# Loading the first batch's q and k as float32 on SyncE, with the casts on chip, in an opening whose order is written anew

## The chip, the cores and the metric

The kernel runs on one core of a Trainium2 chip. Its metric is device time in microseconds of that core, the median of several executions. Engines are named as in the profile: PE (TensorE, matmuls; PEld its weight loads), DVE (VectorE), ACT (ScalarE), POOL (GpSimd), SP (SyncE, which here only issues DMAs).

## The reference

A causal attention with a sliding window of 64 keys over 8 batches, 8 heads, 576 positions and 64 columns a head; its output, as 4608 rows of 512, goes through two dense layers with a gate between them.

```python
scores = scale * q @ k^T                       # scale = 1/8
mask   = (rel >= 0) & (rel < 64)               # rel = row - column
attn   = exp(scores - max) / (sum + 1e-9)      # softmax over masked scores
x      = (attn @ v)  -> (B*S, H*D) = (4608, 512)
h      = x @ w_in                              # 512 -> 2048
g      = h * cos(h)
out    = g @ w_out                             # 2048 -> 512
```

All inputs and the output are float32 in HBM.

## The kernel before

The rows are taken in nine token tiles of 512. For a tile the kernel computes the scores of blocks of 64 rows against the two 64-key chunks that the window touches, the softmax, the value products (`o_ps`, transposed, so that they are the first layer's input `xT`), the first layer in 16 blocks of 128 columns (`h_ps`, L453), the sine (L595) and the gate (L598), and the second layer (`out_ps`, L609). From the second tile on, the attention of a later batch is woven into a tile's two layers: steps are put on a plan with a due time (`at`) and released as the matmuls advance (`pump`).

The opening, up to the first L453 of the second tile, is different. All instructions are issued in program order to the engines' queues (`manual_schedule`), and for the opening that order is the text `FIRST`: a list of step names, each run through the table `steps`. A name carries its arguments, and a last letter `d`, `a`, `p` or `s` says the engine: DVE, ACT, POOL or an SP transfer. The names that matter here:

- `Lq0.p`, `Lk0.p`: load q or k of batch 0 for the pair p of heads. In the kernel before, pair 0 comes as float32 through SP (`load_plain`, L168 to L171) and is cast by `cq`, `ck` (`cast_plain`, the copy itself recorded at L137); pairs 1 to 3 come through POOL, whose DMA casts on the way (`load_heads`, L165). `Lq1`, `Lk1` do the latter for batch 1, `Lv0.c`, `Lv1.c` (L188) load chunks of v, `Lwi.i` and `Lwo.i` quarters of the weights (L204, L207), `Lq2`, `Lk2` chunks of batch 2 (L182).
- `tq`, `tk`, `Tq`, `Tk`: transposes of a pair's rows on PE (L216), put into SBUF by `pq`, `pk`, `Pq`, `Pk` (the copies at L137, or L234 and L236).
- `s`, `m`, `e`, `i`, `n`, `w`, `c`: scores of a group of four row blocks, their maximum, exps (L336), reciprocal, norm (L353), PE transposes (`tw_ps`, L364) and the copy of these (`wT`, L137), for the first tile's eight groups `p.g`. `Gs`, `Gm`, `Ge`, `Gi`, `Gn`, `Gw`, `Gp` are the same for groups 8 to 18, of the second tile; for most of these `Gc` takes the place of `Gw` and `Gp`: a DMA transpose through SP (L367).
- `zA`, `zB`, `zC`, `yA`, `yB`, `y`: the spreading of v's chunks to both halves of the partitions (`spread_v`): a copy, or with `s` an SP transfer (L199).
- `v`, `x`: value products of the first tile, by halves (L403), and their put into `xT`; `h`, `S`, `g`: first layer, sine and gate of the first tile, by halves (L417, L423, L429); `o.q.m`: a quarter of the second layer for 128 rows (L436), `oc` its put; `V`, `X`: value products (L384) and their put for the second tile.
- `ms`: clearing of a pair's block tile `qB` (L546); `io`, `mk`, `mc`: the masks; `tb`, `tb2`: loads of ScalarE's tables.

Every engine works through its own instructions in the order in which the list issued them, and waits there for what each needs.

Of the kernel before, what the change touches and what calls it, by code (L numbers as in the profile page):

```python
# [75 lines left out]
def kernel(  # L76
# [572 lines left out]
```

## Time and profile before

| what | before |
|---|---|
| time, median of 3 runs | 309.11 us (309.06 to 309.75) |
| span of the profiled execution | 306.25 us |
| what lies around the span in that execution (time less span) | 2.86 us, a time of 309.11 us |
| busy share of the span | PE 97%, ACT 76%, DVE 75%, POOL 63% |
| granted PE clock | 1.00 in the stretches read |
| HBM read, written | 36.70 MB, 9.44 MB |

Times in profile rows count from the start of the span. A row of the timeline has its start, its length (of several instructions of one kind in a run, from the first's start to the last's end), the engine, the line, the operation with output and inputs, and in brackets the idle time just before it with what ended it. A row of groups has busy time and mean of one in ns. Since instructions are pipelined, neighbouring rows can overlap a little.

### The profile page before, as it was taken

The numbers are of one execution on the slowest core, as the hardware profiler recorded it, in microseconds if no ns is written. First come the engines' busy times: TensorE is split into PE (matmuls) and PEld (weight loads), VectorE is DVE, ScalarE is ACT, GpSimd is POOL, SyncE is SP. The second block draws the span as 40 slices with busy tenths as digits, with TensorE's granted clock in tenths as the row PEclk, the third lists the DMA queues.
The fourth block names the chain that finished last, engine by engine and source line by source line (L and its number), as shares of the span: only waits on it lengthen the run. The fifth ranks groups of instructions, "written<-read, shape, count | busy, mean of one in ns | idle before, by whom it ended". The sixth has DMA issues, their size and how long they took to land.

```text
span 306.3 us, 7904 instructions
## 1 busy us (share of the span) xinstructions
PE 296.2 (97%) x2616; PEld 159.0 (52%) x2616; DVE 228.5 (75%) x908; ACT 234.3 (76%) x785; POOL 192.5 (63%) x228
## 2 busy tenths in 40 slices
PE   3889999999999999999999999999999999999996
PEld 2768844545555555445544555454545554454443
DVE  5999978599769976798579857986698668235801
ACT  5998799677997799779976997699879986116600
POOL 8998579995659669967998599959903930000000
PEclk9999999999999999999999999999999999999999
DMA  7999999999999995999999999999794643011011
GB/s 146 179 212 192 200 180 130 121 149 191 226 113 116 175 223 80 121 133 232 125 121 137 231 143 104 157 221 148 86 137 107 169 78 141 2 68 71 1 67 70
DMA packets 159945, 42.14 MB, mean 138 GB/s; under 512 B 148256, under 2 KB 155168, under 8 KB 159904
## 3 DMA queue, kind: packets, MB, share of 16 engines
q0 software_dynamic: 100192, 18.06, 80.1%
q1 hardware_dynamic: 59568, 23.38, 40.6%
q8 instruction: 20, 0.33, 0.4%
q14 instruction: 21, 0.17, 0.2%
q10 hardware_dynamic: 144, 0.20, 0.2%
HBM read 36.70 MB, written 9.44 MB: 151 GB/s over the span
## 4 chain that ended last, share of the span: by engine, by line
PE 90%; POOL 4%; DMA 2%; DVE 1%; ACT 1%; issue 1%; POOLq 0%; DVEq 0%; ACTq 0%
PE h_ps L453 35%; PE out_ps L609 35%; PE h_ps L417 5%; PE s_ps L303 4%; PE out_ps L436 4%; PE o_ps L384 3%; DMA k<-in_k_dram 2%; POOL w L353 2%; PE tq_ps L219 1%; POOL v L188 1%; PE out_ps L465 1%; PE s_ps L309 1%; PE tw_ps L364 1%; POOL w_in L204 1%; ACT e L336 1%
## 5 line engine op out<-in xcount | busy, mean ns | idle before, releaser
L609 PE MATMUL out_ps<-w_out,gT 128*128 128x512 bf16 x496 | 117.3, 379 | 0.0
L453 PE MATMUL h_ps<-xT,w_in 128*128 128x512 bf16 x512 | 115.3, 379 | 0.3
L595 ACT ACTIVATE sin<-h_ps 128x512 f32<-128x512 f32 x128 | 73.7, 598 | 32.7 <-PE h_ps L453 31.4
L598 DVE TENSOR_TENSOR gT<-h_ps,sin 128x512 bf16<-128x512 f32 x128 | 82.1, 685 | 21.9 <-ACT sin L595 21.2
L336 ACT ACTIVATE e<-s,negm 128x128 f32<-128x128 f32 (+1 forms) x256 | 97.1, 382 | 0.6 <-DVE negm L324 0.6
L353 POOL TENSOR_TENSOR w<-e,rden 128x512 bf16<-128x512 f32 (+1 forms) x74 | 70.0, 962 | 36.6 <-DVE rden L346 18.8
L453 PEld LDWEIGHTS <-w_in 128*128 128x128 bf16 x512 | 48.8, 98 | 54.7 <-issue 0.4
L609 PEld LDWEIGHTS <-gT 128*128 128x128 bf16 x496 | 45.9, 98 | 44.2
L324 DVE CUSTOM_DVE_ANT_0 s<-s_ps,mask 128x128 f32<-128x128 f32 (+1 forms) x256 | 56.4, 279 | 1.7 <-PE s_ps L309 0.9
L336 ACT ACTIVATION_READ_ACCUMULATOR e<-s,negm 128x1 f32 x256 | 48.3, 189 | 0.0
L182 POOL DMA_DIRECT2D q<-in_q_dram x36 | 28.3, 785 | 10.7 <-DMA q<-in_q_dram 4.0
L188 POOL DMA_DIRECT2D v<-in_v_dram x40 | 34.4, 878 | 0.3 <-issue 0.2
L182 POOL DMA_DIRECT2D k<-in_k_dram x36 | 28.2, 783 | 3.9 <-DMA k<-in_k_dram 1.2
L137 ACT COPY out_sb<-out_ps 128x512 f32<-128x512 f32 (+1 forms) x18 | 10.2, 566 | 24.5 <-PE out_ps L609 18.4
L346 DVE RECIPROCAL rden<-den 128x4 f32<-128x4 f32 (+1 forms) x79 | 13.1, 166 | 19.0 <-ACT e L336 18.6
L303 PEld LDWEIGHTS <-qB 128*128 128x128 bf16 x216 | 16.5, 98 | 14.2
L137 DVE CAST xT<-o_ps 128x512 bf16<-128x512 f32 x24 | 15.5, 677 | 10.1 <-PE o_ps L384 10.1
L137 DVE COPY out_sb<-out_ps 128x512 f32<-128x512 f32 x18 | 12.4, 690 | 13.2 <-PE out_ps L609 12.5
L324 DVE DVE_READ_ACCUMULATOR2_ANT negm<- 128x1 f32 x256 | 21.3, 83 | 0.0
L303 PE MATMUL s_ps<-kT,qB 128*128 128x128 bf16 (+1 forms) x216 | 21.2, 216 | 0.0
L137 POOL COPY v<-v 64x1536 bf16<-64x1536 bf16 (+3 forms) x12 | 18.8, 1570 | 0.3
L137 DVE COPY qB<-tq_ps 64x384 bf16<-64x384 bf16 (+1 forms) x40 | 15.6, 390 | 0.4
(70 smaller groups left out, 257.8 us busy)
## 6 DMA issues: line engine op xcount, KB each, us to landing
out_dram<-out_sb SPq DMA_DIRECT2D x16, 512.0 KB, 7.5
v<-in_v_dram POOLq DMA_DIRECT2D x32, 128.0 KB, 5.7
q<-in_q_dram POOLq DMA_DIRECT2D x36, 96.0 KB, 8.6
k<-in_k_dram POOLq DMA_DIRECT2D x36, 96.0 KB, 8.5
w_in<-in_moe_w_in_dram POOLq DMA_DIRECT2D x4, 512.0 KB, 8.7
w_out<-in_moe_w_out_dram POOLq DMA_DIRECT2D x4, 512.0 KB, 10.8
wT<-w SPq DMA_TRANSPOSE x68, 4.4
q<-in_q_dram POOLq DMA_DIRECT2D x7, 144.0 KB, 6.0
```

The lines of the kernel that those rows point to most:

```text
L137: {"a": nc.scalar.copy, "p": nc.gpsimd.tensor_copy}.get(engine, nc.vector.tensor_copy)(out, in_)
L182: nc.gpsimd.dma_start(out=st[name, b][:, c].rearrange("p (h d) -> p h d", h=H), in_=src.rearrange("h p d -> p h d"))
L188: nc.gpsimd.dma_start(out=vt.rearrange("p (h d) -> p h d", h=H), in_=v[b, :, c * 128:c * 128 + n, :].rearrange("h p d -> p h d"))
L303: nc.tensor.matmul(out=s_ps[:, u, 0:64 * chunks].rearrange("p (a t) -> p a t", a=chunks), lhsT=qblocks[(b % 2) * PAIRS + p][:, j].rearrang ...
L324: nc.vector.tensor_tensor_reduce(out=s[:, u, c], in0=s_ps[:, u, c], in1=mask[:, 2 - j % 2 if j else 0, c], scale=-scale if b else -1.0, sc ...
L336: nc.scalar.activation(e[:, u, c], s[:, u, c], AF.Exp, bias=negm[:, u:u + 1], scale=1.0 if n < n_first else -1.0, accum_out=den[:, u:u + 1])
L353: (nc.gpsimd if engine == "p" else nc.vector).tensor_tensor(out=w[:, 0:u], in0=e[:, 0:u], op=ALU.mult, in1=rden[:, 0:u].unsqueeze(2).to_br ...
L417: nc.tensor.matmul(out=h_ps[:, half * e:half * e + half], lhsT=w_in_sb[:, ks, ff * 128:ff * 128 + 128], rhs=st["xT", 0][:, ks, half * g:ha ...
L453: nc.tensor.matmul(out=st["h", ff], lhsT=w_in_sb[:, ks, ff * 128:ff * 128 + 128], rhs=st["xT", mt][:, ks], start=start, stop=stop)
L595: nc.scalar.activation(sin, h_ps, AF.Sin, bias=math.pi / 2.0)
L598: nc.vector.tensor_tensor(out=gt[:, e], in0=h_ps, in1=sin, op=ALU.mult)
L609: nc.tensor.matmul(out=o_ps[e], lhsT=gT[ff // 2][:, ff % 2, ms * 128:ms * 128 + 128], rhs=w_out_sb[:, ff], start=ff == 0, stop=ff == n_ff - 1)
```

## The change

SP issues all eight loads of batch 0's q and k as float32, each pair of heads one load. Two of them land in tiles of the output pool as before, the other six in a float32 view of the buffer of `w_out`, which is loaded later. All eight are cast on chip: four by DVE (k3, q3, q0, k1), two by ACT (q1, k0), two by POOL (q2, k2). POOL's own list of DMAs begins with v and batch 1. The list of the opening is another one altogether: the pairs are begun with pair 3; POOL clears two of the `qB` tiles ahead of its first load and four more later, where DVE did all; three of the first norms are on POOL and one on DVE; `zA.1` and `y.1` become SP transfers and `zB.0` a POOL copy; the blocks of the first layer come in the order 3, 2, 7, 6, 5 and the quarters of `w_in` in the order 1, 3, 2, 0; `Tk.2` and `Tq.2` stand within the first layer; `Gp.8` and `Gp.15` are on ACT.

```diff
@@ FIRST: the beginning of both lists
-    "io ms.0.d Lq0.0 Lk0.0 ms.1.d mk cq.d ms.2.d mc ck.a tq.0 Lq0.1 pq.0.d Lk0.1 tk.0 pk.0.a s.0.0.0 "
-    "Lq0.2 tq.1 tk.1 m.0.0 pq.1.a ms.3.d s.0.1.1 Lk0.2 tq.2 pk.1.d s.1.0.2 Lq0.3 Lk0.3 tk.2 s.1.1.3 "
...
-    "m.1.1 i.2.0 Pk.0.a e.3.0 Lwi.2 Tk.1 n.1.0.p s.2.1.1 Pq.1.d Gs.10.2 m.2.1 Gs.9.4 n.0.0.p Pk.1.a "
-    "n.2.0.p i.3.0 e.1.1 w.0.0 zA.0.d w.1.0 c.0.0.d Gs.12.0 w.2.0 n.3.0.p i.0.1 c.1.0.d zA.1.d c.2.0.d "
...
+    "ms.5.d ms.3.p io mk ms.7.p mc Lv0.1 Lk1.0 Lq1.0 Lv0.0 Lk0.3 ck.3.d tk.3 pk.3.a Lq0.3 cq.3.d tq.3 "
+    "Lq0.0 cq.0.d tq.0 pq.0.d Lq0.1 Lk0.0 pq.3.a s.3.0.0 m.3.0 Lk0.1 ck.1.d Lk1.1 cq.1.a tq.1 ck.0.a tk.0 "
+    "pk.0.d s.3.1.1 m.3.1 pq.1.a tk.1 pk.1.d e.3.0 i.3.0 s.0.0.2 m.0.0 Lq1.1 Lv0.3 Lq0.2 cq.2.p tq.2 Lk0.2 "
+    "pq.2.d e.3.1 i.3.1 ck.2.p tk.2 pk.2.a s.1.0.3 m.1.0 Tk.0 Pk.0.d e.0.0 e.1.0 s.2.1.4 s.1.1.0 s.2.0.1 "
+    "Tq.0 m.2.1 Lwi.1 m.2.0 e.2.0 Lv0.2 s.0.1.2 Pq.0.d i.0.0 i.1.0 Lwi.3 n.3.0.p w.3.0 c.3.0.d n.1.0.d "
+    "Tq.1 Pq.1.a Tk.1 Pk.1.a i.2.0 m.0.1 zA.0.d Lwi.2 e.0.1 Gs.9.3 w.1.0 c.1.0.d Gs.8.1 n.0.0.p w.0.0 "
+    "c.0.0.d n.2.0.p w.2.0 c.2.0.d Gm.9 zA.1.s v.0.0 x.0.0.a v.1.0 x.1.0.d Gs.12.2 e.2.1 i.0.1 m.1.1 "
...
@@ FIRST: the end of both lists
-    "Gc.13 Lk2.0 Gp.8.d o.3.2 Gi.15 Gw.16 Lk2.1 Ge.17 Lk2.2 o.1.3 Gn.15.d V.0 Gp.16.d oc.2.a Gw.15 Gi.17 "
-    "Lk2.3 o.2.3 V.1 Gp.15.d X.0.a Gn.17.d X.1.d V.2 V.3 X.2.a X.3.d Gc.17 o.3.3 oc.3.a Gs.18.4 Gm.18 "
-    "Ge.18 Lk2.4 Gi.18 Gn.18.d Gc.18 Lk2.5 Lv1.4 "
...
+    "Gm.16 Ge.15 Gi.15 Gn.8.d Gw.8 Gn.15.d Gw.15 o.2.0 oc.3.d Ge.16 Gi.16 Gn.16.d Gm.18 Gw.16 Gp.16.d "
+    "Ge.17 Gi.17 Gp.8.a V.0 X.0.d Gp.15.a Ge.18 o.3.0 oc.0.a V.1 X.1.a V.3 Gc.13 Gi.18 Gn.17.d V.2 X.2.d "
+    "Gn.18.d Gc.18 Lk2.2 Lk2.0 Lk2.1 Lv1.4 X.3.a Gc.17 "
@@
+    stage = w_out_sb.rearrange("p a f -> p (a f)").bitcast(F32)[:, 0:6 * RC * D].rearrange("p (c x) -> p c x", c=6)
@@
-    def load_plain(name):
-        rows = moe.tile([128, 2, d_model], F32, tag="out", name="rows", bufs=OUTS).rearrange("p a f -> p (a f)")[:, 0:RC * D]
-        st["rows", name] = rows
-        nc.sync.dma_start(out=rows, in_={"q": q, "k": k}[name][0, 0:2].rearrange("h (p c) d -> (h p) (c d)", c=RC))
+    def load_plain(name, p):
+        if p:
+            rows = stage[:, 2 * p - 2 + "qk".index(name)]
+        else:
+            rows = moe.tile([128, 2, d_model], F32, tag="out", name="rows", bufs=OUTS).rearrange("p a f -> p (a f)")[:, 0:RC * D]
+        st["rows", name, p] = rows
+        nc.sync.dma_start(out=rows, in_={"q": q, "k": k}[name][0, 2 * p:2 * p + 2].rearrange("h (p c) d -> (h p) (c d)", c=RC))
@@
-    def cast_plain(name, engine):
+    def cast_plain(name, p, engine):
...
-        copy(engine, st[name, 0][:, 0], st.pop(("rows", name)))
+        copy(engine, st[name, 0][:, p], st.pop(("rows", name, p)))
@@ steps
-    steps = {"Lq0": lambda p: load_heads("q", 0, p, 1) if p else load_plain("q"),
-             "Lk0": lambda p: load_heads("k", 0, p, 1) if p else load_plain("k"),
+    steps = {"Lq0": lambda p: load_plain("q", p), "Lk0": lambda p: load_plain("k", p),
```

Lines of the changed kernel stand one lower from L115 on, and three to four lower from L170 on (the first layer L417 is L421 there, L453 is L457, the exps L336 are L340, the norms L353 are L357).

More of the change, by code (lines that the diff above doesn't have):

```diff
@@ L549, in spread_first @@
         return lambda i, engine: spread_v(0, i, engine, lo, hi)
-    steps = {"Lq0": lambda p: load_heads("q", 0, p, 1) if p else load_plain("q"),
-             "Lk0": lambda p: load_heads("k", 0, p, 1) if p else load_plain("k"),
-             "cq": lambda engine: cast_plain("q", engine), "ck": lambda engine: cast_plain("k", engine),
-             "Lq1": lambda p: load_heads("q", 1, p, 1), "Lk1": lambda p: load_heads("k", 1, p, 1),
+    steps = {"Lq0": lambda p: load_plain("q", p), "Lk0": lambda p: load_plain("k", p),
+             "cq": lambda p, engine: cast_plain("q", p, engine), "ck": lambda p, engine: cast_plain("k", p, engine),
+             "Lq1": lambda p, n=1: load_heads("q", 1, p, n), "Lk1": lambda p, n=1: load_heads("k", 1, p, n),
              "Lv0": lambda c: load_v(0, c), "Lv1": lambda c: load_v(1, c), "Lq2": lambda c: load_chunk("q", 2, c), "Lk2": lambda c: load_chunk("k", 2, c),
```

25 rows, old and new, of the table FIRST are left out of this document.

## The prediction

> **What bounds the kernel now.** I read the page's first part, then the busy time of each engine in the first 20 us, then the chain of work that ended last, and TensorE's timeline of the opening.
>
> ```profile
> PE 296.2 (97%) x2616; PEld 159.0 (52%) x2616; DVE 228.5 (75%) x908; ACT 234.3 (76%) x785; POOL 192.5 (63%) x228
> ```
> ```profile
> sum 20.00, PE 13.25 PEld 10.43 DVE 15.95 ACT 15.80 POOL 18.01; mean PE 3.31 PEld 2.61 DVE 3.99 ACT 3.95 POOL 4.50
> ```
> ```profile
> 8.69 3.52 POOL v L188 x4
> 12.21 2.10 POOL w_in L204 x3
> 14.51 4.09 POOL w L353 x4
> 18.65 0.40 PE tw_ps L364 x4
> ...
> 303.43 0.29 DVE last_sb L137
> ```
> ```profile
> 18.98 0.44 PE L403 MATMUL o_ps<-wT,v 128*64 128x64 bf16 x16
> ...
> 21.18 1.93 PE L417 MATMUL h_ps<-xT,w_in 128*128 128x256 bf16 x16
> ...
> 36.67 0.47 PE L216 MATMUL tk_ps<-ident,k 64*64 64x64 bf16 x18
> 36.97 0.73 PE L216 MATMUL tq_ps<-ident,q 64*64 64x64 bf16 x36
> 37.64 1.04 PE L436 MATMUL out_ps<-w_out,gT 128*128 128x512 bf16 x4
> ...
> 53.41 0.44 PE L384 MATMUL o_ps<-wT,v 128*64 128x64 bf16 x16
> 53.79 0.40 PE L364 MATMUL tw_ps<-ident,w 128*128 128x128 bf16 x4
> 54.02 1.03 PE L436 MATMUL out_ps<-w_out,gT 128*128 128x512 bf16 x4
> 54.98 0.95 PE L384 MATMUL o_ps<-wT,v 128*64 128x64 bf16 x48
> 55.86 1.04 PE L436 MATMUL out_ps<-w_out,gT 128*128 128x512 bf16 x4
> 56.83 0.41 PE L309 MATMUL s_ps<-kT,qT 64*64 64x128 bf16 x8
> 57.17 2.76 PE L453 MATMUL h_ps<-xT,w_in 128*128 128x512 bf16 x12
> ```
>
> TensorE is busy for 97% of the span, so only its idle time can be won, and that lies mostly at the start: 13.25 us of the first 20, where GpSimd is busiest with 18.01. The chain says why: GpSimd issues loads until 14.51, then normalises four groups to 18.60, and only then come the last transposes and the first value products (18.98). I use four marks: first value products 18.98, first L417 21.18, first out part 37.64, first L453 57.17. From the last mark on both kernels run the same program, so what the change does to 57.17 it does to the time; the profiled run has 306.25 of span and 2.86 outside it, 309.11, which is the median of the runs.
>
> **GpSimd's queue up to its first norm.**
>
> ```profile
> 1.75 0.75 POOL L165 DMA_DIRECT2D q<-in_q_dram  x1
> ...
> 3.54 0.73 POOL L165 DMA_DIRECT2D k<-in_k_dram  x1
> ```
> ```profile
> L165 POOL DMA_DIRECT2D q<-in_q_dram x5: 533/558/746, 1.7 to 6.7; - x5
> ...
> DMA to landing us min/median/max: 4.7/5.7/6.3
> ```
> ```profile
> L137 POOL COPY v<-v 64x2048 bf16<-64x2048 bf16 x5 | 9.5, 1892 | 0.3
> L137 POOL COPY v<-v 64x1536 bf16<-64x1536 bf16 x5 | 7.3, 1456 | 0.0
> ...
> masks.py:197 POOL MEMSET ident<- 128x128 bf16 x1 | 0.2, 204 | 0.3 <-POOLq L633 0.3
> L633 POOL MEMSET const-bfloat16-1.0<- 128x1 bf16 x1 | 0.1, 101 | 0.0
> ```
> ```profile
> 3.68 0.46 DVE L137 CAST q<-rows 128x576 bf16<-128x576 f32 x1 [0.60 <-DMA rows<-in_q_dram]
> ```
> ```profile
> 4.39 0.67 ACT L137 CAST k<-rows 128x576 bf16<-128x576 f32 x1 [0.20 <-DMA rows<-in_k_dram]
> ```
>
> Added ahead of the first load: two clears of 1,152 columns. GpSimd's memset costs (204 - 101) / 127 = 0.81 ns a column, so 1.03 us each, and the first issue moves from 1.75 to about 3.8. Removed: six of its q, k loads of batch 0; left ahead of the casts are three v loads (3.52 / 4 = 0.88) and four of batch 1 (0.56 less overlap, 0.54), 4.8 us, to 8.6. Then two casts (q2, k2), which wait for SyncE's seventh and eighth load. SyncE's first two landed 0.71 apart (the casts they release start at 3.68 and 4.39), so alone the eighth lands at 3.65 + 7 x 0.71 = 8.6; sharing the engines with GpSimd's loads I take 9.6. No row shows a GpSimd cast; by the copies' slope, (1892 - 1456) / 512 = 0.85 ns, 576 columns and 0.1 of start are 0.6; bounds are DVE's 0.46 and, with a f32 input slower than bf16, 1.0; I take 0.66, near the slope. So the casts end at 10.3. Two w_in issues (2.30 / 3 = 0.77 by the chain) and a v issue follow: first norm possible at 12.7, where it was 14.51. GpSimd is 1.8 us early.
>
> **What is late next: exps, then a copy that goes to SyncE.**
>
> ```profile
> 8.18 0.36 ACT L336 ACTIVATE e<-s_ps,negm 128x128 f32<-128x128 f32 x1
> ...
> 16.80 0.28 ACT L336 ACTIVATION_READ_ACCUMULATOR e<-s_ps,negm 128x1 f32 x1
> ```
> ```profile
> 17.04 2.42 SPq L199 DMA_DIRECT2D v<-v  x3
> ```
>
> The landing times of three lines follow: GpSimd's v loads (L188), SyncE's v<-v copies (L199), SyncE's two f32 loads (L171); then from the page the w_in quarters.
>
> ```profile
> DMA to landing us min/median/max: 5.6/5.7/5.7
> ```
> ```profile
> DMA to landing us min/median/max: 5.9/6.1/6.9
> ```
> ```profile
> DMA to landing us min/median/max: 2.9/3.0/3.2
> ```
> ```profile
> w_in<-in_moe_w_in_dram POOLq DMA_DIRECT2D x4, 512.0 KB, 8.7
> ```
>
> The fourth norm needs the fifth batch of exps. These run from 8.18 to 17.08 now, with two PSUM copies of ScalarE among them, and one in the new order: 16.4. The third GpSimd norm (1.02) then ends at 17.6, a microsecond before 18.60, and its products could start at about 18.2. But zA.1, half of the spreading of v's first chunk, was a VectorE copy and becomes a SyncE transfer. Its source, v0.0, is GpSimd's fourth load, issued at 5.8 and landing 5.7 to 6.3 later, 12.2; the copy takes 5.9 to 6.9 by the three of its kind, so it is there at 18.1 to 19.1; I take 18.7. Both groups of value products run then, 2 x 0.44, and the copy of the second (0.67, as the cast of like size) ends at 20.25: first L417 0.93 early. The w_in quarters that it wants then are there: quarter 1, issued at 10.3, lands by the page 8.7 later at 19.0, quarter 3 at 20.7, two blocks ahead of its use.
>
> **From the first layer to the first L453.** The L417 stage lasts 36.67 - 21.18 = 15.49 now. Into it the new order takes two of the three pair transposes that stand behind it (36.67 to 37.64, 0.97, so 0.65), one batch of scores (57.17 - 56.83 = 0.34) and one group of transposes (54.02 - 53.79 = 0.23): it ends at 20.25 + 15.49 + 1.22 = 36.96, no earlier than now. TensorE's out parts start 0.68 early (37.64 before), yet they aren't what this stage waits for:
>
> ```profile
> L336 ACT ACTIVATE e<-s,negm x36: 333/386/389, 38.8 to 52.0; 128x128 f32<-128x128 f32 x32, 128x64 f32<-128x64 f32 x4
> ```
> ```profile
> L137 ACT COPY wT<-tw_ps 128x512 bf16<-128x512 bf16 x1 | 0.8, 762 | 0.0
> ```
> ```profile
> wT<-w SPq DMA_TRANSPOSE x68, 4.4
> ```
>
> 36 exps run back to back from 38.8 to 52.4, 13.6 us. They start 2.1 behind the end of L417 (last sine, table load), so at 39.1 to 39.3 and end at 52.8. Then the change puts two wT copies (Gp.8, Gp.15) on ScalarE, where one was; Gp.8, on VectorE before and now behind the last of the exps, is what the first V waits for: 0.76, so 53.6, some 0.3 for the matmuls' queue, and up to 0.6 if ScalarE idles once among its batches: V.0 at 53.9 to 54.5 against 53.41, later. Behind V.0 the old order has 57.17 - 53.41 = 3.76; the new one has one out part fewer there (0.97 of pace), no transposes (0.23) and no scores (0.34): 2.2, or 2.4 with a hitch. First L453 then at 56.1 to 56.9. I take 56.67, in the later half, since V.2 waits for transposes through SyncE: the last, of a batch some 2 us before the end of the exps, is issued at about 50.5 and lands 4.4 later (the page's median), 54.9, a microsecond ahead of its use; and y.1, the spreading of 64x2048 of batch 1's v, is now a copy on the same queue, between the third transpose and the fourth. Gain: 57.17 - 56.67 = 0.5.
>
> Costed at nothing: the staging of f32 rows in w_out's buffer (its loads stand behind most norms in GpSimd's list, long after the casts); VectorE's three more casts (0.46 each) and ScalarE's one (0.67), before the first exp, where the profile has VectorE and ScalarE waiting for the loads themselves (0.60 and 0.20 in their rows); clears moved off VectorE; four more clears of 1.03 on GpSimd between 28 and 50, where it isn't on the chain but for one norm. If that cover fails, one norm comes 1.0 late.
>
> **The sum:** 309.11 - 0.5 = 308.6. A measurement of this kernel can tell 0.3%, 0.93 us, from no change: faster lies below 308.18, slower above 310.04.
>
> **Rivals.**
>
> R1, the SyncE copy is quick. SyncE's quiet loads landed in 2.9 to 3.2, half of what its copies took at 17 us beside GpSimd's loads. If zA.1 at 12.2 does the same, the products start at 18.2 at the latest, the second group at about 18.3 instead of 19.14: 0.85 more, 307.7 (307.5 to 307.9). Against it: in that stretch eight of GpSimd's loads are under way.
>
> R2, slower: SyncE's loads are held up by GpSimd's, and GpSimd itself pays, as it waits for them with all its later issues behind the wait. If both queues share the engines evenly once GpSimd's first load moves (an estimate: at 5.8, 2 us behind its issue at 3.8), four f32 loads have landed by then and the other four land 1.42 apart: the eighth at 11.5. The k2 cast ends at 12.2, the w_in quarters 1 and 3 are issued 1.9 late, and with them land late: 12.2 + 8.7 = 20.9 for quarter 1 and 14.6 + 8.7 = 23.3 or more for quarter 3, when the new order of L417 wants them at 20.25 and, two blocks on (1.93, the row of 21.18), at 22.2. TensorE stands for 23.3 - 22.2 = 1.1 us, or 1.7 if quarter 3 is another 0.6 late behind the f32 loads; first L453 at 57.8 to 58.4, the time 309.7 to 310.3, of which I take 310.1. It decides from an eighth landing of about 10.8 on. For it: the 5.7 of the cast loads with only two loads of SyncE beside them. Against: the two kinds aren't one queue. The Trainium skill ("DMA: Bandwidth & Descriptors", Rules for kernel authors) says that spreading DMAs over several issuing engines doesn't help bandwidth, since all run on the same 16 DMA engines. The trace's spacing of 0.71 for SyncE's two loads alone can't settle it.
>
> R3, VectorE's casts hold GpSimd. The issue at 3.54 took 0.73 where its like took 0.56, while the cast of 3.68 to 4.14 ran: 0.17 of loss in 0.46. If three more casts held it fully, GpSimd would lose 1.4 before 8.6; as it waits there until 9.6 anyway for the eighth load, 0.4 or so reaches the products: 309.0. The Trainium skill ("SBUF — State Buffer", SBUF: two separate sides) states that a f32 copy of VectorE within SBUF shuts GpSimd out of a shared port for the whole instruction; here the row shows a loss of about a third of it, and the rule's full price is what R3 gives.
>
> R4, the gain is lost behind the exps: ScalarE idles between two batches, or the last wT transpose takes 5 to 5.5 instead of 4.4 behind the y.1 copy: 309.1 to 309.6.
>
> That the change doesn't do what it says isn't likely: the order is written out by hand and SyncE's first eight instructions are the loads, none with a wait.
>
> **How the numbers follow.** Forecast 0.40 (308.0 to 309.0, about a quarter of it under 308.18), R1 0.19, R2 0.19, R3 0.09, R4 0.13 (a small part over 310.04 where two of its hitches meet). Faster by over 0.3%: 0.19 + 0.09 = 0.28. Slower: 0.19 + 0.04 = 0.23. Within: 0.49. The range takes in R1 and R2, 307.5 to 310.3; the unknown casts' bound of 1.0 each moves GpSimd by 0.7 and lies inside it.
>
> **What would show it.** Right: GpSimd's first issue at 3.8 and first norm at 12.5 to 13; the last of SyncE's eight loads landing before 10; the first value products at 18.5 to 19 released by the v<-v transfer; L417 beginning near 20.2 and ending near 37; exps ending at 52.6 to 53.4; first L453 at 56.1 to 57. Wrong: an eighth f32 load after 10.8, TensorE idle among the L417 blocks with w_in as releaser (R2), products at 18.2 (R1), issues of 0.9 and more under VectorE's casts (R3), or V.2 waiting for a DMA (R4).

## The result, and the profile after

The changed kernel took 311.83 us, median of five runs (311.16 to 313.32); the kernel before took 309.75 beside it (309.06 to 310.05, five runs). The ratio is 1.0091, 95% interval 1.0064 to 1.0118: slower by 0.9%, outside the range of 307.5 to 310.3. The profiled execution is the slowest of the five (span 311.5, time 313.32), so a second profile of the same kernel was taken (`again`: span 309.1, time 310.92; median of its six runs 311.44, ratio 1.0088, interval 1.0060 to 1.0116). Both are read below.

After's busy time in the first 20 us, and one row of five microseconds, whose column before the last two is the granted PE clock:

```profile
sum 20.00, PE 11.70 PEld 9.65 DVE 15.37 ACT 14.85 POOL 16.01; mean PE 2.92 PEld 2.41 DVE 3.84 ACT 3.71 POOL 4.00
...
20.00:25.00 5.00, 4.33 (x56) 3.09 (x56) 4.61 (x24) 4.42 (x24) 4.91 (x7) 0.66 1.23 220
```

GpSimd has 2.0 us less to do in the first 20, as the change meant; TensorE, which should have gained, did 1.55 less. The clock of 0.66 belongs to this execution; in `again` it is 1.00 there. The marks on TensorE's timeline, first of after, then of `again`:

```profile
20.98 1.21 PE L407 MATMUL o_ps<-wT,v 128*64 128x64 bf16 x32 [0.41 <-DVE wT L138]
...
23.52 2.56 PE L421 MATMUL h_ps<-xT,w_in 128*128 128x256 bf16 x16
...
40.44 1.89 PE L440 MATMUL out_ps<-w_out,gT 128*128 128x512 bf16 x7
...
58.41 0.47 PE L388 MATMUL o_ps<-wT,v 128*64 128x64 bf16 x16 [0.86 <-DVE rden L350]
...
61.28 1.03 PE L457 MATMUL h_ps<-xT,w_in 128*128 128x512 bf16 x4 [0.16 <-issue]
```
```profile
20.44 1.07 PE L407 MATMUL o_ps<-wT,v 128*64 128x64 bf16 x32 [0.41 <-DVE wT L138]
...
22.29 1.91 PE L421 MATMUL h_ps<-xT,w_in 128*128 128x256 bf16 x16
...
38.70 1.89 PE L440 MATMUL out_ps<-w_out,gT 128*128 128x512 bf16 x8
...
56.67 0.47 PE L388 MATMUL o_ps<-wT,v 128*64 128x64 bf16 x16 [0.86 <-DVE rden L350]
...
59.00 2.76 PE L457 MATMUL h_ps<-xT,w_in 128*128 128x512 bf16 x12
```

| mark, us | before | forecast | `again` | after |
|---|---|---|---|---|
| first exp | 8.18 | as before | 9.09 | 10.01 |
| first value products | 18.98 | 18.7 | 20.44 | 20.98 |
| first L421 (L417) | 21.18 | 20.25 | 22.29 | 23.52 |
| first out part | 37.64 | 36.96 | 38.70 | 40.44 |
| V.0 | 53.41 | 53.9 to 54.5 | 56.67 | 58.41 |
| first L457 (L453) | 57.17 | 56.67 | 59.00 | 61.28 |

In `again` the steps from V.0 on are as forecast (2.33 for 2.2 to 2.4; 2.87 in after), and the miss is made before the first L421: 2.04 of the 2.33 us that it is late against the forecast at its last mark. Other profiles of the new order lose more behind the first L421; the part on the tail comes back to that.

**Where it goes in the opening.** VectorE's and GpSimd's timelines of `again`, in order of time:

```profile
2.83 0.29 DVE L148 TENSOR_TENSOR mask<-mask 128x128 f32<-128x128 f32 x1 [1.33 <-POOL mask L144]
3.16 0.84 DVE L149 TENSOR_SCALAR mask<-mask 128x128 f32<-128x128 f32 x1
...
4.29 0.63 DVE L151 COPY mask<-mask 128x64 f32<-128x64 f32 x1
4.47 0.74 DVE L138 CAST k<-w_out 128x576 bf16<-128x576 f32 x1
...
8.48 0.89 DVE L138 CAST k<-w_out 128x576 bf16<-128x576 f32 x1
...
17.00 1.38 DVE L357 TENSOR_TENSOR w<-e,rden 128x512 bf16<-128x512 f32 x1
18.30 0.17 DVE L350 RECIPROCAL rden<-den 128x4 f32<-128x4 f32 x1
```
```profile
2.86 1.06 POOL L550 MEMSET qB<- 128x1152 bf16 x1
3.86 1.07 POOL L192 DMA_DIRECT2D v<-in_v_dram  x1
...
9.04 0.85 POOL L138 CAST q<-w_out 128x576 bf16<-128x576 f32 x1
9.91 0.67 POOL L138 CAST k<-w_out 128x576 bf16<-128x576 f32 x1
10.53 0.77 POOL L208 DMA_DIRECT2D w_in<-in_moe_w_in_dram  x1
...
12.93 1.07 POOL L357 TENSOR_TENSOR w<-e,rden 128x512 bf16<-128x512 f32 x1
...
16.79 1.03 POOL L357 TENSOR_TENSOR w<-e,rden 128x512 bf16<-128x512 f32 x1 [2.06 <-DVE rden L350]
18.54 2.08 POOL L357 TENSOR_TENSOR w<-e,rden 128x512 bf16<-128x512 f32 x2 [0.72 <-DVE rden L350]
```

Read the lengths of VectorE's rows against GpSimd's ends. The mask step of 3.16 took 0.84 and ended with the memset (3.92) and a little; the copy of 4.29 took 0.63 and ended at 4.92, with the DMA issue (4.93); the norm of 17.00 took 1.38, which is the 0.82 until GpSimd's norm ends at 17.82 and 0.56 of its own. In the profile of before mask steps took 0.23, the cast 0.46 and VectorE's norms 0.7. So in these rows a VectorE instruction that works from SBUF to SBUF waits until GpSimd's clear, norm or v issue is over. It is not so beside every issue: the casts of 5.14 and 5.50 of `again` took 0.44 and 0.46 while GpSimd issued k and q loads, and the mask steps of before (0.23) ran beside such issues too. And the wait spreads: the reciprocal of the fifth batch stands behind that norm until 18.30, so GpSimd's next norm comes at 18.54 and the value products after 20.

### The profile page after: what moved, and what is told of

Same layout as the page of the kernel before. It is cut to its first block, busy times and chain, and to the rows that moved or that the text cites. A ratio compares the mean times of both kernels' runs of the same rounds, so it can differ in the third digit from the quotient of the medians.

```text
span 311.5 us, 7879 instructions
## 1 busy us (share of the span) xinstructions
PE 294.9 (95%) x2583; PEld 160.6 (52%) x2616; DVE 229.7 (74%) x907; ACT 236.1 (76%) x788; POOL 192.3 (62%) x225
## 3 DMA queue, kind: packets, MB, share of 16 engines
HBM read 36.70 MB, written 9.44 MB: 148 GB/s over the span
## 4 chain that ended last, share of the span: by engine, by line
PE 71%; DMA 9%; DVE 6%; ACT 5%; POOL 4%; issue 3%; SPq 2%; POOLq 0%
PE h_ps L457 31%; PE out_ps L612 27%; DMA wT<-w 4%; PE s_ps L307 3%; DMA kT<-k 3%; ACT e L340 3%; PE h_ps L421 3%; POOL w L357 2%; PE o_ps L388 2%; DMA rows<-in_q_dram 2%; DVE gT L433 1%; POOL v L138 1%; PE out_ps L469 1%; PE tq_ps L223 1%; DVE negm L323 1%
## 5 line engine op out<-in xcount | busy, mean ns | idle before, releaser
L612 PE MATMUL out_ps<-w_out,gT 128*128 128x512 bf16 x482 | 114.6, 379 | 0.8 <-issue 0.2
L457 PE MATMUL h_ps<-xT,w_in 128*128 128x512 bf16 x497 | 114.3, 379 | 1.0 <-issue 0.2
L340 ACT ACTIVATE e<-s,negm 128x128 f32<-128x128 f32 (+1 forms) x256 | 97.1, 382 | 0.4 <-DVE negm L328 0.4
L357 POOL TENSOR_TENSOR w<-e,rden 128x512 bf16<-128x512 f32 (+1 forms) x68 | 64.2, 961 | 40.1 <-DVE rden L350 36.9
L457 PEld LDWEIGHTS <-w_in 128*128 128x128 bf16 x512 | 48.8, 98 | 54.5 <-issue 0.2
L340 ACT ACTIVATION_READ_ACCUMULATOR e<-s,negm 128x1 f32 x256 | 48.1, 188 | 0.0
L138 DVE CAST xT<-o_ps 128x512 bf16<-128x512 f32 x24 | 15.7, 682 | 12.7 <-PE o_ps L388 12.4
L138 DVE COPY out_sb<-out_ps 128x512 f32<-128x512 f32 x19 | 13.1, 688 | 12.5 <-PE out_ps L612 12.5
L328 DVE DVE_READ_ACCUMULATOR2_ANT negm<- 128x1 f32 x256 | 21.3, 83 | 0.0
L138 POOL COPY v<-v 64x1536 bf16<-64x1536 bf16 (+3 forms) x13 | 19.9, 1527 | 0.3
```

What stands on the lines that cost most here:

```text
L138: {"a": nc.scalar.copy, "p": nc.gpsimd.tensor_copy}.get(engine, nc.vector.tensor_copy)(out, in_)
L328: nc.vector.tensor_tensor_reduce(out=s[:, u, c], in0=s_ps[:, u, c], in1=mask[:, 2 - j % 2 if j else 0, c], scale=-scale if b else -1.0, sc ...
L340: nc.scalar.activation(e[:, u, c], s[:, u, c], AF.Exp, bias=negm[:, u:u + 1], scale=1.0 if n < n_first else -1.0, accum_out=den[:, u:u + 1])
L357: (nc.gpsimd if engine == "p" else nc.vector).tensor_tensor(out=w[:, 0:u], in0=e[:, 0:u], op=ALU.mult, in1=rden[:, 0:u].unsqueeze(2).to_br ...
L457: nc.tensor.matmul(out=st["h", ff], lhsT=w_in_sb[:, ks, ff * 128:ff * 128 + 128], rhs=st["xT", mt][:, ks], start=start, stop=stop)
L612: nc.tensor.matmul(out=o_ps[e], lhsT=gT[ff // 2][:, ff % 2, ms * 128:ms * 128 + 128], rhs=w_out_sb[:, ff], start=ff == 0, stop=ff == n_ff - 1)
```

## The experiments

All ratios are to the kernel before, on the chip of that run, with their 95% intervals. The marks are those of the one profile of each run.

| run | median us | ratio, interval | first exp | first products | first L457 |
|---|---|---|---|---|---|
| `again` | 311.44 | 1.0088 (1.0060 to 1.0116) | 9.09 | 20.44 | 59.00 |
| `clears_later` | 314.64 | 1.0177 (1.0146 to 1.0209) | 9.37 | 20.96 | 61.44 |
| `score_first` | 312.03 | 1.0099 (1.0076 to 1.0122) | 11.19 | 21.98 | 60.99 |
| `loads_alone` | 312.66 | 1.0147 (1.0105 to 1.0190) | 10.09 | 22.04 | 60.26 |
| `loads_held` | 311.41 | 1.0051 (1.0023 to 1.0079) | 9.18 | 21.20 | 61.24 |
| `order_alone` | 313.39 | 1.0100 (1.0065 to 1.0136) | 9.86 | 20.97 | 60.68 |
| `norms_pool` | 311.79 | 1.0076 (1.0048 to 1.0104) | 10.01 | 20.14 | 60.23 |
| `iotas_first` | 312.38 | 1.0086 (1.0055 to 1.0117) | 9.00 | 21.17 | 60.70 |
| `tail_back` | 315.62 | 1.0200 (1.0156 to 1.0243) | 9.08 | 20.44 | 66.47 |
| `all_three` | 315.03 | 1.0161 (1.0125 to 1.0197) | 8.86 | 19.70 | 64.22 |
| `gp8_back` | 311.30 | 1.0064 (1.0038 to 1.0090) | 9.08 | 20.45 | 60.55 |
| `old_y1_sync` | 310.09 | 1.0011 (0.9986 to 1.0036) | 8.53 | 19.88 | 58.14 |
| `early_exp` | 311.72 | 1.0068 (1.0035 to 1.0102) | 8.71 | 20.70 | 60.43 |
| `mended` | 312.30 | 1.0085 (1.0051 to 1.0119) | 8.26 | 20.52 | 60.62 |
| `mended_k1` | 311.33 | 1.0046 (1.0024 to 1.0069) | 8.27 | 19.72 | 59.98 |
| `casts_vector` | 315.93 | 1.0201 (1.0166 to 1.0236) | 9.18 | 24.44 | 63.91 |

**`again`**: no edit.

> The changed kernel itself, a second profile of it. The first profile is of its slowest execution (313.32, median 311.83), with a granted PE clock of 0.50 from 22 to 24 us and a wT transpose of 6.7 us before the last value products. Theory A (the loss sits in the opening's order and loads, the same in every execution): first f32 load of q0 lands after 6 us again, first exp at 9.8 to 10.2, first value products at 20.5 to 21, first L457 at 59.5 to 61. Rival B (the loss is mostly the clock dip and the slow transpose, which come and go): in a profile without a dip the first L457 comes before 58.5.

The marks lie near theory A's, a little better (the load of q0 landed at 5.3, not after 6), and the clock doesn't dip: of 4.1 us of delay against the kernel before at the last mark in the first profile, 1.8 are there in the better one. The dip and a slow transpose were on top of that in the first profile. Nor is the dip the loss by the times: six executions of the changed kernel with a granted clock of 0.994 or 0.995 have a median of 311.71, the five with 0.999 or 1.00 one of 311.83. It does come back in profiles below that have the new order (0.66 in five microseconds of early_exp and of iotas_first); none of the four profiles with the old order has it in its first 60 us.

**`clears_later`**

```diff
-    "ms.5.d ms.3.p io mk ms.7.p mc Lv0.1
+    "ms.5.d io mk mc Lv0.1
-    h.0.7.2 h.0.6.1 ms.4.d n.1.1.d
+    h.0.7.2 h.0.6.1 ms.4.d ms.3.d ms.7.d n.1.1.d
```

> The two clears at the head of GpSimd's list (2 x 1.06 us) go to VectorE behind ms.4, so iotas and GpSimd's loads come some 2 us earlier and VectorE's mask steps find no GpSimd memset beside them. Theory A (what binds is the third f32 load, q0, and the cast and transposes behind it): masks earlier by about 1.8 us, first exp earlier by 0.3 at most, time 311.3 to 311.9. Theory C (GpSimd's clears bind: late masks, late v0.0, VectorE shut out while GpSimd works): first exp earlier by 1 us or more and the time 310.0 to 310.8. If GpSimd's earlier loads slow the f32 loads down: q0 lands later than 6.5 and the time is 312 or more.

The third outcome, slower still. The masks did come 1.5 us earlier, and the eighth f32 load landed at 11.9 instead of 9.9: the clears at GpSimd's head are also a delay that lets SyncE's loads go first. But in this profile, of the fastest execution (312.53), that is not where most of the loss is. The first L421 came at 22.52, only 0.2 later than in `again`; then TensorE waited for a norm of VectorE, which now stood behind three clears (25.30 to 27.05):

```profile
27.65 0.62 PE L368 MATMUL tw_ps<-ident,w 128*128 128x128 bf16 x8 [1.16 <-DVE w L357]
```

`again` has no such wait, so the 314.64 holds a cost of the edit itself.

**`score_first`**

```diff
-    "Lq0.0 cq.0.d tq.0 pq.0.d Lq0.1 Lk0.0 pq.3.a s.3.0.0 m.3.0 Lk0.1
+    "Lq0.0 Lq0.1 Lk0.0 pq.3.a s.3.0.0 m.3.0 cq.0.d tq.0 pq.0.d Lk0.1
```

> Only the order of VectorE's and TensorE's steps: the first group's scores and maximum (s.3.0, m.3.0) go ahead of the cast and the transposes of q0, so they don't wait for the third f32 load. Theory A: first exp at about 8.8 instead of 10.0 and all behind it about 1 us earlier, if ScalarE then finds the next groups in time; time 310.6 to 311.2. Theory D (the middle of the opening binds, VectorE's list from 15 to 21 us with a norm, a v copy and the wT copies, however early the exps begin): first exp earlier, first value products within 0.4 of 21, time 311.4 to 312.

The edit missed its aim: ScalarE's list still had the copy of q1's transposes ahead of the exps, and these now came later. ScalarE's timeline:

```profile
10.64 0.65 ACT L238 ACTIVATE qT<-tq_ps 128x576 bf16<-128x576 bf16 x1 [2.32 <-PE tq_ps L220]
11.19 0.36 ACT L340 ACTIVATE e<-s_ps,negm 128x128 f32<-128x128 f32 x1
```

A step moved on one engine needs all engines' lists read; `early_exp` below does it.

**`loads_alone`** and **`loads_held`**: the old order with the new loads. The second moves the clears of two pairs from VectorE to GpSimd's head.

```diff
 (loads_alone, against the kernel before)
-    "io ms.0.d Lq0.0 Lk0.0 ms.1.d mk cq.d ms.2.d mc ck.a tq.0 Lq0.1 ...
+    "io ms.0.d Lq0.0 Lk0.0 Lq0.1 Lk0.1 Lq0.2 Lk0.2 Lq0.3 Lk0.3 Lq1.0 Lk1.0 Lq1.1 Lk1.1 Lv0.0 Lv0.1 Lv0.2 Lv0.3 ms.1.d mk cq.0.d ...
...
 (loads_held, against loads_alone)
-    "io ms.0.d Lq0.0 ... ms.2.d ... ms.3.d ...
+    "io ms.0.d ms.2.p ms.3.p Lq0.0 ...
```

> The order of the kernel before, with the change of the loads alone: all eight q, k loads of batch 0 through SyncE as f32, in the order of use, GpSimd's loads of batch 1 and v directly behind the iotas, casts on VectorE (q0, q1), ScalarE (k0, k1) and GpSimd (q2, k2, q3, k3). Theory A (order and loads both cost): f32 loads land 0.7 us apart with a gap at 4 to 6 us as in the changed kernel; GpSimd issues w_in by 11 us instead of 12.2, norms 0.5 to 1 us earlier, time 308.5 to 309.5. Theory E (the loads are the whole loss, f32 rows are twice the bytes at HBM's side and the casts crowd the engines): time 311 or more with this order too.

> The kernel with the old order and all eight f32 loads of SyncE again (as in loads_alone), but GpSimd clears two qB tiles ahead of its first DMA, as the changed kernel does, so that its DMAs begin 2 us later. Theory S (two queues with transfers under way take turns, so GpSimd's early loads double the spacing of SyncE's; in loads_alone they landed 1.5 us apart, in the changed kernel 0.7 to 0.9): f32 loads 0.7 to 0.9 apart, the eighth at 9.8 to 10.5 instead of 14.0, w_in issued at about 11 instead of 14.7, time 309.5 to 310.7 against 312.7. Rival (the f32 bytes and the casts cost it, not the turns): eighth load after 12, time 312 or more.

The landing times of SyncE's f32 loads, of `again` and of loads_alone, and GpSimd's timeline, first loads_alone, then loads_held:

```profile
DMA to landing us min/median/max: 2.8/4.6/5.8
```
```profile
DMA to landing us min/median/max: 3.0/7.8/10.0
```
```profile
10.55 0.67 POOL L138 CAST q<-w_out 128x576 bf16<-128x576 f32 x1 [2.91 <-DMA w_out<-in_q_dram]
12.03 0.67 POOL L138 CAST k<-w_out 128x576 bf16<-128x576 f32 x1 [0.81 <-DMA w_out<-in_k_dram]
13.22 0.67 POOL L138 CAST q<-w_out 128x576 bf16<-128x576 f32 x1 [0.52 <-DMA w_out<-in_q_dram]
14.08 0.67 POOL L138 CAST k<-w_out 128x576 bf16<-128x576 f32 x1 [0.20 <-DMA w_out<-in_k_dram]
14.70 2.25 POOL L208 DMA_DIRECT2D w_in<-in_moe_w_in_dram  x3
```
```profile
9.86 0.75 POOL L138 CAST q<-w_out 128x576 bf16<-128x576 f32 x1
...
11.69 0.73 POOL L138 CAST k<-w_out 128x576 bf16<-128x576 f32 x1
12.30 1.55 POOL L208 DMA_DIRECT2D w_in<-in_moe_w_in_dram  x2
```

Where GpSimd's DMAs start at 1.75, SyncE's loads land at half their pace, as if the two queues took turns: the casts, which wait for f32 loads, start 1.5 and 1.2 apart. Held back to 3.9, GpSimd finds the loads landed and casts without waiting; w_in is issued 2.4 us earlier. Theory S holds in that. Yet with GpSimd held the loads still cost about half a per cent in the old order (the time, 311.41, is above the forecast of 309.5 to 310.7), so they bring nothing there. Theory E's bytes aren't on HBM's side: 36.70 MB are read in before and in loads_alone alike.

**`order_alone`**: the new order with the old kind of loads for pairs 0 to 2, and with the two clears of GpSimd's head on VectorE, as in clears_later.

```diff
-    "ms.5.d ms.3.p io mk ms.7.p mc Lv0.1 Lk1.0 Lq1.0 Lv0.0 Lk0.3 ck.3.d ...
+    "ms.5.d io mk mc Lk0.3 Lq0.3 Lq0.0 Lk0.0 Lk0.1 Lq0.1 Lq0.2 Lk0.2 Lv0.1 Lk1.0 Lq1.0 Lv0.0 ck.3.d ...
-    h.0.7.2 h.0.6.1 ms.4.d n.1.1.d
+    h.0.7.2 h.0.6.1 ms.4.d ms.3.d ms.7.d n.1.1.d
-    steps = {"Lq0": lambda p: load_plain("q", p), "Lk0": ...
+    steps = {"Lq0": lambda p: load_plain("q", p) if p == 3 else load_heads("q", 0, p, 1), "Lk0": ...
```

> The changed kernel's order with the old kind of loads: only pair 3, which it begins with, comes as f32 through SyncE with VectorE's casts; pairs 0 to 2 come through GpSimd with the cast in the DMA, issued ahead of v and batch 1; no other casts, and the two clears of the head on VectorE later. Theory O (the new order costs by itself: VectorE held by GpSimd, the fifth batch of exps needed first, w_in in an order that leaves no slack): 310.5 or more, first value products after 20. Theory L (the loads cost, the order is as good as the old one): 308.5 to 309.7.

Theory O: the time is above 310.5 and the first products come after 20, though by 0.97 only. By the ratio the new order costs as much without the new loads as with them, but TensorE waits for VectorE's clears here as well (1.17 at 26.5 us). Without that wait, 0.6% would be left (an estimate: 1.17 of the 3.1 us of loss taken off). VectorE's timeline is also a control of the waits: with GpSimd issuing q and k loads beside them instead of clears and a v load, the same mask steps and the cast are short, and the norm, beside a GpSimd norm, is as long as in `again`:

```profile
2.16 0.36 DVE L149 TENSOR_SCALAR mask<-mask 128x128 f32<-128x128 f32 x1
...
2.81 0.25 DVE L151 COPY mask<-mask 128x64 f32<-128x64 f32 x1
...
3.71 0.46 DVE L138 CAST k<-w_out 128x576 bf16<-128x576 f32 x1 [0.63 <-DMA w_out<-in_k_dram]
...
17.52 1.38 DVE L357 TENSOR_TENSOR w<-e,rden 128x512 bf16<-128x512 f32 x1
```

**`norms_pool`**, **`iotas_first`**, **`tail_back`**, **`all_three`**

```diff
 (norms_pool)
-    m.2.1 Lwi.1 ... Pq.0.d i.0.0 i.1.0 Lwi.3 n.3.0.p w.3.0 c.3.0.d n.1.0.d ... Lwi.2 e.0.1 ... n.0.0.p
+    m.2.1 i.0.0 Lwi.1 ... Pq.0.d i.1.0 Lwi.3 n.3.0.p w.3.0 c.3.0.d ... Lwi.2 n.0.0.p n.1.0.p e.0.1 ...
 (iotas_first)
-    ms.5.d ms.3.p io mk ms.7.p mc
+    ms.5.d io ms.3.p mk ms.7.p mc
 (tail_back)
-    y.1.s ... Gi.17 Gp.8.a V.0
+    y.1.d ... Gi.17 Gp.8.d V.0
```

> From the changed kernel: the norm n.1.0 from VectorE to GpSimd, behind Lwi.2 and n.0.0, and the reciprocal i.0.0 earlier, so that GpSimd needn't stand from 14.7 to 16.8. Theory F (what binds from 15 to 21 us is VectorE, which is held by GpSimd: its norm of 0.63 took 1.38 beside a GpSimd norm, its v copy of 0.3 to 0.5 took 0.76): first value products at 18.7 to 19.3 instead of 20.4, time 310.0 to 310.7 against 311.4. Theory A (the late first exp binds, and the norms follow it however they are dealt out): products at 20 or later, time 311 to 311.6. If the SyncE copy zA.1 is then the last to come: products at 18.2 to 18.5 at the earliest, released by a DMA.

> From the changed kernel: the iotas of the masks ahead of GpSimd's two clears; GpSimd's first DMA stays where it is (3.85). Masks then begin at 1.83 on VectorE instead of 2.83, ScalarE's mask casts at about 3.6 instead of 5.0. Theory C (late masks and casts hold the opening): the cast of k3 ends by 4.1 instead of 5.2, first exp at 8.3 to 8.7 instead of 9.1, time 310.6 to 311.0. Theory A' (the third f32 load and the casts of q1 and k0 hold it, which land at 6.7 and 7.6 whatever the masks do): first exp at 8.9 to 9.1, time 311.2 to 311.6.

> From the changed kernel: Gp.8 and y.1 back on VectorE, as before the change. Theory G (the exps' end and the wT copy on ScalarE behind them hold V.0, as the forecast had it at 0.3 to 0.8): V.0 earlier by 0.3 to 0.7 measured from the last exp, time 310.8 to 311.1. Theory H (VectorE is as late as ScalarE there, and y.1 costs it 1.12 in front of its norms): no gain, 311.3 to 312.

> The three edits together. If the losses add up (theories F, C, G): 309.0 to 310.0, V.0 at 54.3 to 55.2 and the first L457 at 56.8 to 57.8, about as the kernel before. If a single wait holds all (theory A): 310.8 or more.

norms_pool and iotas_first are not to be told from the changed kernel. In norms_pool the products came at 20.14, theory A's place, the first exp being at 10.01 in that profile; but they came 2.28 behind the end of the fifth batch of exps, where it is 3.03 in `again`. So the norm's price was real, but it did not reach the time (the part on the tail says where it went). In iotas_first the first exp stayed at 9.0: theory A', and theory C falls. tail_back and all_three are slower by about another per cent: one y.1 copy on VectorE, at the place where this order has it, runs beside GpSimd's copies and clears, a norm behind it took 1.81, and TensorE stands 3 us for what waits behind both. (In this profile the granted clock also dips, to 0.58 from 20 to 25 us.) VectorE and TensorE of tail_back:

```profile
52.00 1.72 DVE L138 COPY v<-v 64x2048 bf16<-64x2048 bf16 x1
```
```profile
57.38 4.37 PE L440 MATMUL out_ps<-w_out,gT 128*128 128x512 bf16 x12 [3.12 <-DVE negm L328]
```

**`gp8_back`** and **`old_y1_sync`**

```diff
 (gp8_back, against the changed kernel)
-    Gi.17 Gp.8.a V.0
+    Gi.17 Gp.8.d V.0
 (old_y1_sync, against the kernel before)
-    Ge.15 y.1.d Gn.14.p ... Gc.12 Gm.17
+    Ge.15 Gn.14.p ... Gc.12 y.1.s Gm.17
```

> The changed kernel with the copy Gp.8 alone back on VectorE (y.1 stays a SyncE transfer), to part the two edits of tail_back, which took 315.6. If y.1 on VectorE was the whole loss there (a copy of 1.73 beside GpSimd, in front of the norms and scores of the last groups): 311.0 to 311.8, V.0 earlier by up to 0.4 against the last exp. If Gp.8 holds VectorE too: 312.5 or more.

> The kernel before the change with one edit: y.1, a VectorE copy of 1.12 us on its chain of work at 48.6, goes through SyncE behind the third transpose. If that copy bound the end of the opening: V.0 0.3 to 0.8 earlier than 53.4, time 0.3 to 0.8 below the kernel before. If the transfer (about 6 us) or the transposes behind it come last instead: equal or up to 1 slower.

gp8_back is as fast as the changed kernel, so y.1, alone or together with Gp.8, was the loss in tail_back; V.0 came 0.4 later after the last exp, not earlier. old_y1_sync is not to be told from the kernel before. Its opening up to 45 us is that of the kernel before, and in its profile (time 311.67, the slowest of its twelve) the first products came at 19.88 and L417 at 22.19: about 1 us is what one execution differs from another by itself, and no mark above is worth more than that without its ratio.

**`early_exp`**, **`mended`**, **`mended_k1`**, **`casts_vector`**

```diff
 (early_exp)
-    "Lq0.0 cq.0.d tq.0 pq.0.d Lq0.1 Lk0.0 pq.3.a s.3.0.0 m.3.0 Lk0.1 ... m.3.1 pq.1.a tk.1 pk.1.d e.3.0
+    "Lq0.0 cq.0.d Lq0.1 Lk0.0 pq.3.a s.3.0.0 tq.0 m.3.0 pq.0.d Lk0.1 ... m.3.1 e.3.0 pq.1.a tk.1 pk.1.d
 (mended: early_exp, iotas_first and norms_pool together; mended_k1: mended with)
-    m.3.0 pq.0.d Lk0.1 ck.1.d
+    m.3.0 Lk0.1 ck.1.d pq.0.d
 (casts_vector, against the changed kernel)
-    cq.2.p ... ck.2.p
+    cq.2.d ... ck.2.d
```

> From the changed kernel: on TensorE s.3.0 goes ahead of tq.0, on ScalarE the exps of e.3.0 go ahead of the copy pq.1, the cast of q0 stays where it is. Theory A (the first group's scores wait for the third f32 load and ScalarE for a copy, and all else follows the first exp): first exp at 8.2 to 8.5 instead of 9.1 to 10.0, first value products 0.5 to 1 earlier (19.5 to 20), ratio to the kernel before 1.004 to 1.006 where the changed kernel has 1.009. Theory D (VectorE, GpSimd and the w_in landings from 15 to 25 us bind whatever the first exp does): first exp early, L421 still from 22.2 on, ratio 1.008 or more.

> early_exp with the iotas ahead of the clears and with n.1.0 on GpSimd and i.0.0 early (norms_pool). If the terms add up: first exp at 7.5 to 8.2, first value products at 18.4 to 19, first L421 at 20.2 to 21, ratio to the kernel before 0.998 to 1.003. If something behind the first value products binds (w_in landing at 18.4, 22.4 and 25.4, v copies of SyncE): products early, L421 stage ending after 38.5 all the same, ratio 1.006 or more.

> mended with one VectorE step earlier: the cast of k1 ahead of the copy pq.0, so that it starts at about 8.2, half a microsecond or more before GpSimd's casts. Theory F (VectorE's copies within SBUF wait out GpSimd's work, and this wait is what ate the earlier first exp): cast of k1 in 0.46 to 0.95, second group's exps in step with the first, first value products at 18.8 to 19.6 instead of 20.5, ratio 1.002 to 1.006. Rival D (what lies behind the products binds): products earlier, ratio 1.008 again.

> From the changed kernel: GpSimd's casts of q2 and k2 to VectorE (0.46 each if nothing holds them). Theory F: the cast of k1 falls from 0.89 to 0.46 to 0.6, GpSimd issues w_in 1.4 us earlier, at 9.1, so that the quarters land earlier too; VectorE has 0.5 more to do: first value products 20.0 to 20.6, ratio 1.006 to 1.009. If VectorE is simply full from 8 to 21 us: products at 20.8 or later, ratio 1.009 to 1.012.

early_exp had its first exp at 8.71, later than forecast and earlier than `again`; its products, at 20.70, came no earlier, as the same norm of VectorE stood before them, and its ratio settles nothing between the two theories. mended had its first exp at 8.26, as before the change, and won nothing either. Its VectorE, GpSimd and TensorE say why:

```profile
8.81 1.93 DVE L138 CAST k<-w_out 128x576 bf16<-128x576 f32 x1
```
```profile
9.07 0.73 POOL L138 CAST q<-w_out 128x576 bf16<-128x576 f32 x1
9.68 0.73 POOL L138 CAST k<-w_out 128x576 bf16<-128x576 f32 x1
```
```profile
10.79 0.69 PE L220 MATMUL tk_ps<-ident,k 64*64 64x64 bf16 x18 [1.00 <-DVE k L138]
```

A cast of 0.46 waited out a DMA issue (to 9.13) and two GpSimd casts (to 10.41), which follow one another without a gap, and TensorE waited for it. In mended_k1 the same cast starts 0.66 earlier, ahead of the v issue (8.21) and of the two casts (from 9.10), and is short, although issues of q and v loads run beside it:

```profile
8.15 0.45 DVE L138 CAST k<-w_out 128x576 bf16<-128x576 f32 x1
```

The products came at 19.72 instead of 20.52 (19.6 at the latest was forecast), and the ratio, 1.0046, is the least of the new order's and in the range of theory F, though its interval still overlaps those of mended and `again`. It is slower than the kernel before. In casts_vector theory F's part holds: the cast of k1 took 0.46, and w_in was first issued at 8.97. All the same it is the bad outcome and more: VectorE reaches the two casts only at 12.2 and 14.1, TensorE stands for both, 1.82 and 1.42, and its granted clock is 0.50 from 15 to 20 us.

```profile
12.86 0.47 PE L220 MATMUL tq_ps<-ident,q 64*64 64x64 bf16 x18 [1.82 <-DVE q L138]
14.74 0.69 PE L220 MATMUL tk_ps<-ident,k 64*64 64x64 bf16 x18 [1.42 <-DVE k L138]
```

So GpSimd's two casts are better where they were; what they cost there is the cast of VectorE beside them.

## Why the prediction was wrong

**GpSimd's queue: right.** In `again`: first issue forecast at 3.8 (3.86), eighth f32 load at 9.6 (9.86; 10.49 in after), casts ending at 10.3 (10.58), first norm at 12.7 (12.93). GpSimd was 1.6 us early, and that was worth nothing.

**The fifth batch of exps at 16.4, from "the first exp as now": the first failing step.** The forecast put VectorE's three casts and ScalarE's one at nothing, "before the first exp, where the profile has VectorE and ScalarE waiting for the loads themselves". The idle time of those rows is less than the 1.38 of three casts. The first exp came at 9.09 and 10.01 (9.08 to 10.01 in gp8_back, tail_back and norms_pool, whose lists are the same up to there; 8.18 and 8.53 in before and old_y1_sync). On ScalarE two casts and three copies stand ahead of the first exps, and the last of them waits for TensorE's transposes of q1 (the rows of `again`):

```profile
8.54 0.65 ACT L238 ACTIVATE qT<-tq_ps 128x576 bf16<-128x576 bf16 x1 [0.21 <-PE tq_ps L220]
9.09 0.36 ACT L340 ACTIVATE e<-s_ps,negm 128x128 f32<-128x128 f32 x1
```

while the first scores stand on TensorE behind the third f32 load. early_exp took that away and brought the first exp to 8.71; with the masks early it was 8.26. So the first exp was 0.9 late, put at 0. But that by itself is not what the products lost: in mended_k1 the first exp came at 8.27, and the fifth batch still ended at 17.43, as in `again` (17.41). The copy that had stood ahead of the exps now stood among them, and in both profiles the fifth batch waited for its maximum from VectorE. The rows of `again`, ScalarE and TensorE:

```profile
15.99 0.37 ACT L340 ACTIVATE e<-s_ps,negm 128x128 f32<-128x128 f32 x1 [0.48 <-DVE negm L323]
```
```profile
14.65 0.37 PE L297 MATMUL s_ps<-mask,ident 64*64 64x512 bf16 x1 [0.86 <-issue]
```

TensorE paused in the middle of that batch's scores, for 0.86 here, 0.99 in mended_k1 and 1.41 in iotas_first, and the profile shows nothing that it waited for. The old order has such a pause too (0.92), in transposes, and ScalarE did not wait behind it. The forecast had the batches follow one another without such a wait. The term that it mis-sized is thus the end of the fifth batch, 17.4 instead of 16.4; how this 1.0 divides among the late beginning, the copies and the pause stays open.

**The norm of VectorE: the second.** The change gave VectorE a norm, for which the forecast has no term at all, and three more casts, which it took at 0.46 each. Beside GpSimd the norm took 1.38 instead of about 0.7, and two of the casts 0.74 and 0.89. With the norm the reciprocal of the fifth batch came at 18.30, where the batch had ended at 17.4; the third GpSimd norm, forecast to end at 17.6, ended at 19.58. What the norm costs the products is shown by experiment: from the end of the fifth batch to the first products it is 3.03 to 3.05 in after, `again`, early_exp, gp8_back and order_alone, and 2.28 or 2.29 in norms_pool, mended and mended_k1, where GpSimd does that norm. These two steps, 1.0 and about 0.8, are most of the 2.04 of delay at the first L421.

**R3 named the right port and the wrong side.** The forecast let VectorE's casts hold GpSimd's issues and put 0.4 on it. The rows show mostly the reverse: VectorE's instructions grow by up to 1.5 us, GpSimd's by 0.2 in the opening of `again` (1.07 for a v issue of 0.89, 0.85 for a cast of 0.67) and by up to 0.5 elsewhere (a copy of v, 64x1024, took 1.05 in `again` and 1.58 in mended_k1). The Trainium skill ("SBUF — State Buffer", SBUF: two separate sides) calls the pair of ports an exclusive lock for the whole instruction, taken by whichever starts first. By that rule either can wait; the 1.93 of mended and the 1.38 of the norm are what it gives with GpSimd first, and beside GpSimd's casts and norms the trace agrees with it in full, not by "about a third". Beside its DMA issues it doesn't always: VectorE's 0.23 to 0.46 in order_alone went through.

**R2's mechanism is real, but the change is built to avoid it.** loads_alone shows the turns (loads 1.5 apart, casts to 14.7), clears_later some of it (11.9). In the changed kernel the two clears hold GpSimd back. The forecast read them as a delay only.

**The SyncE copy, the forecast's binding step, wasn't late.** Forecast at 18.7, it landed at 18.2 in `again`, with 5.2 us for itself; VectorE's wT copies (the releaser in the products' row) came 2 us behind it. R1 so had nothing to win. In early_exp, where it was issued at 14.7, it landed at 21.1 and held the products for another 0.2.

**The tail: right in size in `again` alone.** There L421 lasted 16.41 (16.71 forecast), and V.0 to L457 took 2.33. The second tile's exps lasted 14.1 (13.6 forecast), and 1.5 passed from their end to V.0 (1.1 to 1.7). R4's late transpose came in the first profile (0.2 us of TensorE at the last products), not in `again`. After the last mark the forecast had no difference; `again` has 1.0 from a wait of one later batch, which the profile of before has not (TensorE's waits):

```profile
PE s_ps L307 <- DMA kT<-k: 1.0, 1, 1.0
```

gp8_back has 248.85 behind that mark, less than the 249.08 of before, so I count this as scatter and not as the change's doing.

From the first out part to the first L457 the forecast has 19.7. Of the old order's profiles before, old_y1_sync and loads_alone have 19.4 to 19.5, and loads_held has 21.3, with a wait for a wT transpose in it. `again` has 20.3, after 20.8, and norms_pool, mended and mended_k1, which had won at the products, 21.3 to 21.8. The rows of mended_k1, VectorE and TensorE, show what took the gain away:

```profile
49.30 2.16 DVE L357 TENSOR_TENSOR w<-e,rden 128x512 bf16<-128x512 f32 x1
```
```profile
52.30 2.76 PE L440 MATMUL out_ps<-w_out,gT 128*128 128x512 bf16 x12 [1.31 <-DVE negm L328]
```

This norm, too, stood behind GpSimd: behind a copy of v (49.42 to 50.03) and a k issue (to 50.78), after which it ran for its own 0.68. In `again` the same norm took 0.94, and TensorE waited 0.25 for the maxima behind it. So the exps of the second tile last 15.2 from first to last, instead of 14.1. It is the wait of the opening in a second place, and it eats the 0.75 that GpSimd's norm had won. That is read from the traces; no run moves this norm, so what is left of mended_k1's half a per cent without it stays open.

## What to carry to other kernels

Price an instruction by what runs beside it: in these runs a VectorE copy or norm from SBUF to SBUF could cost its own time plus what is left of GpSimd's instruction, and of those that follow it without a gap, so work dealt out to both in the same microseconds isn't always work in parallel. When a step is freed on one engine (here GpSimd, 1.6 us early), ask who is last in the stage now; the engine that was nearly full before (VectorE, with 4.7 of 5 us from 10 us on) is the candidate, and what is added to it is paid (the norm: 0.75 at the products). Then look for the same wait further on: what is won in one place can be lost in the next. And before counting a clear or another filler at a queue's head as a loss, ask whose transfers it lets pass.

## What the runs showed of the hardware

A VectorE cast of 128x576 took 0.46 with GpSimd idle (clears_later), 0.45 beside issues of a q and a v load (mended_k1), and 1.93 behind the end of a v issue and two casts of GpSimd (mended). A memset of GpSimd lengthened VectorE's mask step from 0.23 to 0.84; issues of q and k loads left such steps at 0.23 to 0.36. On GpSimd's side the most seen was 0.5, for a copy of v in mended_k1. With GpSimd's loads under way, SyncE's f32 loads landed 1.5 us apart instead of 0.7, but its eight loads, begun 3 us ahead of GpSimd's first, landed by 9.9 at a pace of 0.7 to 0.9 for the last five. GpSimd's cast of 128x576 from f32 took 0.66 to 0.93, its memset of 1152 columns 1.06. The same opening instructions differed by about 1 us from one execution to another.
